# Attention with pooled keys and a gated MLP: the main keys of the values, loaded 64 keys by two heads per transfer in place of two heads by 64 keys

## The chip, the cores and the metric

The kernel runs on one core of one Trainium2 chip. The time is the device time of one execution in microseconds, as the median of several executions; three of the kernel before are shown. Beside these there is one profiled execution, from which every duration below comes.

## The reference, cut to what matters

Eight batches (B) of eight heads (H) with 576 tokens (S) of 64 numbers (D), all float32. Keys and values are first averaged over groups of 8 tokens, which leaves 72 pooled keys for each head; attention of the 576 queries over the 72 pooled keys gives a 576 x 512 array for each batch, and a gated MLP follows it.

```python
k_p = k.reshape(B, H, Sp, pool, D).mean(axis=3)          # pool = 8, Sp = 72
v_p = v.reshape(B, H, Sp, pool, D).mean(axis=3)
scores = scale * np.matmul(q, k_p.transpose(0, 1, 3, 2))
attn = softmax(scores)
x = np.matmul(attn, v_p)                                 # then (B, S, H * D) = (8, 576, 512)
h = np.maximum(x @ w_in, 0.0)                            # 1024 columns
u, v = h[..., :512], h[..., 512:]
v_n = (v - mean(v)) / sqrt(var(v) + 1e-06)
v_s = np.einsum('ts,bsd->btd', w_spatial, v_n) + b_spatial[None, :, None]
return (u * v_s) @ w_out
```

## The kernel before, in words

The work of one batch is cut into named steps, each a Python generator that records a few instructions at a time: K (load and pool the keys), V (the same for the values), Q (load queries), S (scores and softmax), T and Y (bring the softmax weights into the layout of the next product), A (weights times values, into `xT`), and for the MLP v, u, s and o. The long string `ORDER` at the top of the file lists which step records its next piece. That list alone sets the order of the instructions on every engine and of the transfers on the queue: each engine runs its instructions in this order, and nothing overtakes. Batches overlap: while the MLP of one batch runs on PE, K, V, Q, S and T of the next ones run on the other engines.

All transfers are issued by the sync engine (SP; its rows read SPq) in that one order. The ones that matter here:

- V of batches 2 to 7 (`att_values`, from line 471): the 64 main pooled keys of the eight heads are 8 x 64 rows of 8 x 64 numbers, so 512 numbers or 2 KB each, contiguous in memory for one pooled key. They come in as two tiles `st` of 128 partitions x 2 x 512 from a ring of three buffers that K, V and the weights share. Partition i * 64 + p, slot e holds pooled key p of head 4r + 2i + e. Each tile is filled by two transfers (line 477), so there are four for a batch and 24 in all, of 256 KB each. POOL then adds the eight rows of each group (L307, L312).
- K of batches 2 to 7 (line 422): the same sizes; a transfer takes 64 keys by two heads into 128 partitions, partition 2 * key + head.
- The eight left-over pooled keys of each head (`load_rest`, line 335): 64 partitions, 128 KB.
- Q (line 536), 72 KB in each transfer, four for a pair of heads.
- T goes through memory: DVE transposes the weights into X and XR (L676, L680), SP writes them to `xd` and `xdr` (L683, L686) and reads them back as `pt` (L690) and `pt_r` (L694); ACT and DVE then split `pt_r` into `pt_rr` (L637, L639), and PE multiplies (A, L751 and L754). Y does the same for the last 64 tokens, through `xdl` and `xdlr` (L727 to L737).
- o: ACT copies a result into one of two buffers `ob` (L895), SP stores it (L898). Step v uses the same two buffers for a temporary (`t2`, L824).

Batches 0 and 1 load their keys and values in another way (`first_keys`, `first_values`), which the change leaves alone.

Of the kernel before, what the change touches and what calls it, by code (L numbers as in the profile page):

```python
# [99 lines left out]
def pooled_attention_gmlp(ctx: ExitStack, tc: tile.TileContext, q, k, v, w_in, w_sp, b_sp, w_out, out):  # L100
    nc = tc.nc
# [17 lines left out]
    KM = P // 2  # L119
# [51 lines left out]
    def ring(tag, bufs, shape, dt, name, pool=pl):  # L171
        return pool.tile(shape, dt, name=name, tag=tag, bufs=bufs)
# [130 lines left out]
    def pool_sum(st, dst, eng=nc.vector):  # L303

        w = POOL * D // 2
        while w > D:
            eng.tensor_tensor(st[:, :, :w], st[:, :, :w], st[:, :, w:2 * w], op=ALU.add)  # L307
            w //= 2
        x, y = st[:, :, :w], st[:, :, w:2 * w]
        if len(dst.shape) == 4:  # L310
            x, y = (t.unsqueeze(2).broadcast_to(dst.shape) for t in (x, y))
        eng.tensor_tensor(dst, x, y, op=ALU.add)  # L312

    def pool_half(sts, alt):

        if "%" in alt:
            for st in sts:
                x = st[:, :, :POOL * D // 2]
                eng = nc.vector if "^" in alt else nc.gpsimd
                eng.tensor_tensor(x, x, st[:, :, POOL * D // 2:], op=ALU.add)  # L320
                yield

    def pool_pe(st, dst, alt):

        m, n = dst.shape[0], POOL // 2 if "%" in alt else POOL
        for j in range(n):
            nc.tensor.matmul(dst, lhsT=ident[:m, :m], rhs=st[:, :, j * D:(j + 1) * D], start=j == 0, stop=j == n - 1)

    def ps_pool():
        return ps_big()[:, :(NG + 1) * D].rearrange("p (g d) -> p g d", d=D)  # L330

    def load_rest(src):

        st = ring("kvr", 1, [2 * RR, 1, POOL * D], F32, "st_r")
        nc.sync.dma_start(out=st[:, 0, :], in_=src[:, KM * POOL:, :].rearrange("h (s j) d -> h s (j d)", j=POOL))
        return st

    def rest_engine(alt, pe):

        if pe:  # L340
            return nc.vector if "~" in alt else nc.gpsimd if "!" in alt else None
        return nc.gpsimd if alt else nc.vector
# [43 lines left out]
    def first_values(b, vp, vq):  # L386

        rows = v[b, :, :KM * POOL, :].rearrange("(j i e) (p f) d -> i j p e (f d)", j=2, i=2, f=POOL // 2)
        sts = []
        for h in range(2):  # L390
            sts.append(ring("kv", 3, [P, NG, POOL // 2 * D], F32, "st"))
            for j in range(2):
                nc.sync.dma_start(out=sts[h][:, 2 * j:2 * j + 2, :], in_=rows[h, j])
            yield
        rest = load_rest(v[b])
        yield
        acc = ps_pool()
        for j in range(POOL // 2):
            for h in range(2):
                nc.tensor.matmul(acc[h * KM:(h + 1) * KM, :NG, :], lhsT=pairs, rhs=sts[h][:, :, j * D:(j + 1) * D],  # L400
                                 start=j == 0, stop=j == POOL // 2 - 1)
        yield
        pool_pe(rest, acc[:2 * RR, NG:, :], "")
        yield
        nc.scalar.copy(vp, acc[:, :NG, :])
        nc.scalar.copy(vq, acc[:2 * RR, NG:, :])
        yield
# [54 lines left out]
    def att_values(t, b, alt=""):  # L462

        eng = nc.gpsimd if alt else nc.vector
        vp = ring("vp", 2, [P, NG, D], F32, "vp")
        vq = pl.tile([2 * RR, 1, D], F32, name="vq", tag="vq")
        vr_s = pl.tile([RR, NG, 2, D], F32, name="vr_s", tag="vr_s")
        t["v"] = vp, vr_s
        if b < PE_B:
            yield from first_values(b, vp, vq)  # L470
        else:
            sts, g2 = [], [slice(2 * r, 2 * r + 2) for r in range(2)]
            keys = v[b, :, :KM * POOL, :].rearrange("(r i e) (p j) d -> r e i p (j d)", r=2, i=2, j=POOL)
            for r in range(2):
                sts.append(ring("kv", 3, [P, 2, POOL * D], F32, "st"))
                for e in range(2):
                    nc.sync.dma_start(out=sts[r][:, e, :], in_=keys[r, e])
                yield
            st = load_rest(v[b])
            yield  # L480
            pe = "^" in alt or "%" in alt
            yield from pool_half((*sts, st)[:2 if rest_engine(alt, True) else 3], alt)
            for r in range(2):
                if pe:
                    acc = acc if r else ps_pool()
                    pool_pe(sts[r], acc[:, g2[r], :], alt)
                else:
                    pool_sum(sts[r], vp[:, g2[r], :], eng)
                yield
            by = rest_engine(alt, pe)  # L490
            if by is not None:
                pool_sum(st, vq, by)
            else:
                pool_pe(st, acc[:2 * RR, NG:, :], alt)
            if pe:
                yield
                nc.scalar.copy(vp, acc[:, :NG, :])
                if by is None:
                    nc.scalar.copy(vq, acc[:2 * RR, NG:, :])
                yield  # L500
        for j in range(2):
            rs = slice(j * RR, (j + 1) * RR)
            nc.vector.tensor_tensor(vr_s[:, 2 * j:2 * j + 2, :, :].rearrange("p i e d -> p (i e) d"),
                                    vq[rs].broadcast_to([RR, 4, D]),
                                    mask[rs].unsqueeze(2).broadcast_to([RR, 4, D]), op=ALU.mult)
# [258 lines left out]
    def attention(b):  # L764

        t = {}
        st = {
            "K": lambda **alt: att_keys(t, b, **alt),
            "KT": lambda **alt: att_keys_t(*t["k"], **alt) if b >= PE_B else iter(()),
            "V": lambda **alt: att_values(t, b, **alt),  # L770
            "W": lambda: att_values_split(*t["v"]),
        }
        for g in range(NG):
            st[f"Q{g}"] = lambda g=g, **alt: att_q(t, b, g, **alt)
            st[f"S{g}"] = lambda g=g, **alt: att_softmax(t, b, g, **alt)
        for j in range(NG // 2):
            st[f"T{j}"] = lambda j=j, **alt: att_pt(t, b, j, **alt)
            st[f"Y{j}"] = lambda j=j, **alt: att_pt_l(t, b, j, **alt)
            for half in range(2):
                st[f"A{half}{j}"] = lambda half=half, j=j: att_av(t, half, j)  # L780
        return st, t
# [185 lines left out]
```

## Time and profile before

| | us |
|---|---|
| median of 3 executions | 621.76 |
| lowest and highest | 621.35, 624.94 |
| the profiled execution | 623.88 |
| its span | 622.1 |
| PE busy within the span | 541.8 |
| mean granted clock of PE | 0.942 |

PE is the TensorE matmul, PEld its weight load, DVE the VectorE, ACT the ScalarE, POOL the GpSimd. The profiled execution's time is its span and 1.8 us around it. PEclk and "granted clock" are shares of full speed: 1.00 is 2.4 GHz and 0.50 is 1.2 GHz. "DMA share" is the mean busy share of the core's 16 DMA engines. In rows of a timeline, the figure in square brackets is how long the engine was idle just before the row, and the name behind the arrow is what ended that idle time.

### The profile page before, as it was taken

Reading aid. Unit: us, or ns where it says so; the run is one execution under the profiler, and the core shown is the slowest. Engines: PE = TensorE matmul, PEld = TensorE weight load, DVE = VectorE, ACT = ScalarE, POOL = GpSimd, SP = SyncE. Lnnn points to the kernel's source line nnn. Section 1 sums busy time; section 2 is a strip of 40 time slices with the busy share of each in tenths; the row PEclk is TensorE's granted clock in tenths of the full one; section 3 lists DMA queues with packets and bytes.
Section 4 is the critical chain, followed back from the end, with each engine's and each line's share of the span. In section 5 each row is a group of like instructions: output and inputs, shape, how many; then the busy total and the mean of one; then the engine's idle time right before and its main releaser. Section 6 shows DMA issues by size and latency. Waiting matters only on the chain.

```text
span 622.1 us, 12097 instructions
## 1 busy us (share of the span) xinstructions
PE 541.8 (87%) x4514; PEld 465.6 (75%) x4514; DVE 330.1 (53%) x723; ACT 269.7 (43%) x875; POOL 286.8 (46%) x389
## 2 busy tenths in 40 slices
PE   4899999917963888969799999989769999999998
PEld 3678888916942677858688888768659888988996
DVE  4898989805730437735683576444255654234210
ACT  3589685403720225614545356144144534333322
POOL 2354778815740734843656644224515644221331
PEclk9999999977976797998899999989969999999999
DMA  8986535423144544332645623352232032200002
GB/s 219 271 240 148 133 73 120 103 77 72 45 113 115 152 133 88 92 99 93 142 101 151 148 47 83 110 141 67 77 100 80 3 105 90 70 18 17 35 2 84
DMA packets 122587, 63.12 MB, mean 101 GB/s; under 512 B 81184, under 2 KB 106272, under 8 KB 122528
## 3 DMA queue, kind: packets, MB, share of 16 engines
q1 hardware_dynamic: 122528, 62.35, 38.4%
q8 instruction: 35, 0.57, 0.4%
q14 instruction: 24, 0.20, 0.1%
HBM read 44.92 MB, written 17.40 MB: 100 GB/s over the span
## 4 chain that ended last, share of the span: by engine, by line
PE 65%; DMA 11%; DVE 7%; SPq 6%; POOL 5%; ACT 5%; issue 1%; ACTq 0%; DVEq 0%; POOLq 0%
PE mm L865 14%; PE mm L804 13%; PE mm L891 12%; PE mm L847 12%; DMA out<-ob 4%; PE s_ps L611 2%; PE mm L820 2%; PE tp L751 2%; DMA pt_r<-xdr 2%; PE tp L754 2%; DMA qt<-in_q 2%; ACT e L587 2%; SPq L536 2%; DMA st<-in_k 1%; SPq L694 1%
## 5 line engine op out<-in xcount | busy, mean ns | idle before, releaser
L847 PE MATMUL mm<-xT,win_h 128*128 128x256 f32 (+1 forms) x512 | 104.9, 299 | 4.9 <-DVE vv L827 4.6
L879 POOL TENSOR_TENSOR gT<-g,gT 128x256 fp32r<-128x256 f32 x64 | 47.6, 750 | 125.1 <-ACT gT L876 125.1
L804 PE MATMUL mm<-win_h,xT 128*128 128x512 f32 x256 | 85.7, 417 | 13.6 <-ACT ob L895 9.3
L847 PEld LDWEIGHTS mm<-xT,win_h 128*128 128x128 f32 x512 | 84.6, 191 | 8.0 <-DVE vv L827 5.1
L865 PE MATMUL mm<-wT_h,vn_h 128*128 128x320 f32 (+1 forms) x256 | 77.8, 304 | 9.0 <-ACT ob L895 9.0
L891 PE MATMUL mm<-wout_h,gT 128*128 128x512 f32 (+1 forms) x264 | 80.7, 388 | 0.0
L865 PE MATMUL mm<-wT_l,vn_h 128*128 128x320 f32 (+1 forms) x256 | 77.1, 301 | 0.0
L865 PE MATMUL mm<-wT_h,vn_l 128*128 128x320 f32 (+1 forms) x256 | 77.0, 301 | 0.0
L847 PE MATMUL mm<-xT,win_l 128*128 128x320 f32 (+1 forms) x256 | 76.0, 297 | 0.0
L870 DVE TENSOR_TENSOR g<-mm,ru 128x320 f32<-128x320 f32 (+1 forms) x64 | 28.4, 453 | 82.3 <-PE mm L867 56.9
L804 PEld LDWEIGHTS mm<-win_h,xT 128*128 128x128 f32 x256 | 49.9, 201 | 25.3 <-ACT ob L895 9.5
L594 POOL TENSOR_TENSOR e<-e,rs 128x720 f32<-128x720 f32 (+1 forms) x32 | 41.2, 1287 | 49.9 <-DVE rs L592 47.5
L791 POOL TENSOR_TENSOR rstd<-rstd,neg_half 128x1 f32<-128x1 f32 (+1 forms) x40 | 24.7, 623 | 81.3 <-DVE rstd L789 81.2
L865 PEld LDWEIGHTS mm<-wT_h,vn_h 128*128 128x128 f32 x256 | 49.8, 195 | 10.3 <-ACT ob L895 9.7
L587 ACT ACTIVATE e<-s_ps,mx 128x72 f32<-128x72 f32 x174 | 52.8, 334 | 10.7 <-DVE mx L573 10.6
L891 PEld LDWEIGHTS mm<-wout_h,gT 128*128 128x128 f32 x264 | 48.2, 188 | 9.8
L804 PE MATMUL mm<-win_l,xT 128*128 128x512 f32 x128 | 52.9, 413 | 0.0
L785 DVE BATCH_NORM_STATS2 st<-vv 128x6 f32<-128x512 f32 (+1 forms) x40 | 27.2, 681 | 48.0 <-ACT vv L808 43.8
L814 POOL TENSOR_TENSOR vn_l<-vv,vn_h 128x512 fp32r<-128x512 f32 x32 | 42.0, 1328 | 21.7 <-ACT vn_h L812 21.7
L307 POOL TENSOR_TENSOR st<-st 128x512 f32<-128x512 f32 (+1 forms) x44 | 45.1, 1025 | 13.8 <-DMA st<-in_k 8.6
L891 PE MATMUL mm<-wout_l,gT 128*128 128x512 f32 (+1 forms) x132 | 51.4, 389 | 0.0
L865 PEld LDWEIGHTS mm<-wT_h,vn_l 128*128 128x128 f32 x256 | 49.8, 195 | 0.5
(171 smaller groups left out, 1142.7 us busy)
## 6 DMA issues: line engine op xcount, KB each, us to landing
st<-in_k SPq DMA_DIRECT2D x32, 256.0 KB
st<-in_v SPq DMA_DIRECT2D x32, 256.0 KB
out<-ob SPq DMA_DIRECT2D x31, 256.0 KB
qt<-in_q SPq DMA_DIRECT2D x104, 72.0 KB
xd<-X SPq DMA_DIRECT2D x24, 256.0 KB
pt<-xd SPq DMA_DIRECT2D x24, 256.0 KB
stw<-in_moe_w_in SPq DMA_DIRECT2D x8, 512.0 KB
st<-in_moe_w_out SPq DMA_DIRECT2D x4, 512.0 KB
```

The costliest lines, as they stand in the source:

```text
L307: eng.tensor_tensor(st[:, :, :w], st[:, :, :w], st[:, :, w:2 * w], op=ALU.add)
L587: nc.scalar.activation(em[:, h, :], sv[:, h % 2, h // 2, :], AF.Exp, bias=mx[:, h:h + 1], scale=QK, accum_out=sm[:, h:h + 1])
L594: nc.gpsimd.tensor_tensor(em, em, rs.unsqueeze(2).broadcast_to([P, n, SP]), op=ALU.mult)
L785: nc.vector.bn_stats(st6[:m], vv[:m])
L791: nc.gpsimd.tensor_tensor(rstd[:m], rstd[:m], neg_half[:m], op=ALU.pow)
L804: nc.tensor.matmul(a, lhsT=xT[:, i, o + c * P:o + (c + 1) * P], rhs=w[:, i, DH:], start=(i == 0 and j == 0), stop=(i == NK - 1 and j == 2))
L814: nc.gpsimd.tensor_tensor(t["vn_l"][:, c, :], vv, f32(t["vn_h"][:, c, :]), op=ALU.subtract)
L847: nc.tensor.matmul(a, lhsT=w[:, i, d * P:(d + 1) * P], rhs=xT[:, i, o + ts.start:o + ts.stop], start=(i == 0 and j == 0), stop=(i == NK - ...
L865: nc.tensor.matmul(a, lhsT=x[:, c, ds], rhs=y[:, c, ts], start=(c == 0 and j == 0), stop=False)
L870: nc.vector.tensor_tensor(g, a, t["ru"][:, d, ts], op=ALU.mult)
L879: nc.gpsimd.tensor_tensor(dst[:, d, 1, at:at + m], g[:, o:o + m], f32(dst[:, d, 0, at:at + m]), op=ALU.subtract)
L891: nc.tensor.matmul(a, lhsT=src[:, i, x, at:at + m], rhs=w[:, i, cols], start=(i == 0 and j == 0), stop=(i == ND - 1 and j == 2))
```

## The change

The two transfers that fill a tile of values no longer take one slot e each for all 128 partitions; each takes one half of the partitions (one i) with both slots.

```diff
             for r in range(2):
                 sts.append(ring("kv", 3, [P, 2, POOL * D], F32, "st"))
-                for e in range(2):
-                    nc.sync.dma_start(out=sts[r][:, e, :], in_=keys[r, e])
+                for i in range(2):
+                    nc.sync.dma_start(out=sts[r][i * KM:(i + 1) * KM], in_=keys[r, :, i].rearrange("e p f -> p e f"))
                 yield
```

KM is 64. On the side of the memory a transfer was a loop over 2 heads, in it 64 keys, in it 512 numbers, and went to 128 partitions of 512 numbers. Now it is a loop over 64 keys, in it 2 heads, in it 512 numbers, and goes to 64 partitions of 2 x 512 numbers. Bytes (256 KB), the number of transfers (24), the pieces of 2 KB and the place of every number in the tile are the same.

On PE, DVE, ACT and POOL no instruction and no place in the order differs. (Near 270 us and 285 us PE gets two buffers of the ring `mm` the other way round: a group of L865 there waits for DVE and no longer for ACT, the L450 behind it the reverse, and two rows of L751 exchange their waits for PE and DVE.) On SP the order is the same too; only the shape of L477 differs. The queue of SP around the first V of this kind (batch 2), before: shapes are partitions x pieces x numbers.

```order
L536 DMA qt<-in_q 32x18x32 x4
L477 DMA st<-in_v 128x1x512 x2
L690 DMA pt<-xd 128x4x128 x2
L477 DMA st<-in_v 128x1x512 x2
L694 DMA pt_r<-xdr 32x4x128 x2
L536 DMA qt<-in_q 32x18x32 x8
L335 DMA st_r<-in_v 64x1x512
```

The same place in the change:

```order
L536 DMA qt<-in_q 32x18x32 x4
L477 DMA st<-in_v 64x2x512 x2
L690 DMA pt<-xd 128x4x128 x2
L477 DMA st<-in_v 64x2x512 x2
L694 DMA pt_r<-xdr 32x4x128 x2
L536 DMA qt<-in_q 32x18x32 x8
L335 DMA st_r<-in_v 64x1x512
```

Nothing moved; `pt_r` still stands behind four transfers of values. A little further on, four transfers of values (batch 3) stand together; in the change this piece of SP's queue reads:

```order
L737 DMA pt_r<-xdlr 32x2x32 x2
L477 DMA st<-in_v 64x2x512 x4
L727 DMA xdl<-XL 4x16x128 x2
L730 DMA xdlr<-XLR 64x32
L898 DMA out<-ob 128x512
L683 DMA xd<-X 8x16x512
```

Here too only the shape of L477 is another (before, 128x1x512).

## Rows read from the trace of the kernel before

**Rows 1.** The head of the page: busy time, share of the span and instructions of each engine.

```profile
PE 541.8 (87%) x4514; PEld 465.6 (75%) x4514; DVE 330.1 (53%) x723; ACT 269.7 (43%) x875; POOL 286.8 (46%) x389
```

**Rows 2.** PE in order of time: the rows with more than 1 us of idle time before them, from 100 us on (start, duration, operation; in brackets the idle time and what ended it).

```profile
143.93 0.48 PE L450 MATMUL tp<-ident,kp 128*128 128x128 f32 x1 [17.13 <-ACT ru L850]
181.96 0.58 PE L865 MATMUL mm<-wT_h,vn_h 128*128 128x256 f32 x1 [6.11 <-ACT ob L895]
201.44 1.08 PE L751 MATMUL tp<-pt,vp 64*64 64x256 f32 x2 [10.65 <-DMA pt<-xd]
204.94 0.70 PE L751 MATMUL tp<-pt,vp 64*64 64x256 f32 x3 [2.42 <-DVE xT L183]
235.94 0.58 PE L847 MATMUL mm<-xT,win_h 128*128 128x256 f32 x1 [4.64 <-DVE vv L827]
272.62 0.39 PE L865 MATMUL mm<-wT_h,vn_h 128*128 128x256 f32 x1 [1.39 <-ACT ob L895]
276.01 0.33 PE L450 MATMUL tp<-ident,kp 128*128 128x128 f32 x1 [1.36 <-POOL kp L312]
279.65 0.48 PE L451 MATMUL tp<-ident,kr 128*128 128x128 f32 x1 [3.32 <-POOL kr L312]
305.32 0.69 PE L804 MATMUL mm<-win_h,xT 128*128 128x512 f32 x1 [3.74 <-DVE g L870]
399.92 0.42 PE L865 MATMUL mm<-wT_h,vn_h 128*128 128x320 f32 x1 [1.52 <-ACT ob L895]
414.65 0.58 PE L754 MATMUL tp<-pt_rr,vr 96*128 96x256 f32 x1 [1.41 <-DVE pt_rr L639]
456.75 0.79 PE L804 MATMUL mm<-win_h,xT 128*128 128x512 f32 x1 [9.32 <-ACT ob L895]
```

**Rows 3.** Busy time of each engine, the granted clock of PE (the column 0.50), DMA share and GB/s in the eight stretches after 100 us in which PE had half its clock: the first, the fifth, the sixth, and the sum of the eight (start:end, length, then PE, PEld, DVE, ACT, POOL).

```profile
131.40:148.50 17.10, 4.57 (x23) 3.35 (x27) 2.12 (x5) 3.03 (x8) 2.85 (x3) 0.50 0.36 79
...
278.20:285.00 6.80, 5.35 (x79) 5.12 (x83) 1.67 (x4) 1.93 (x6) 2.08 (x4) 0.50 0.30 95
305.50:308.90 3.40, 3.40 (x9) 2.63 (x10) 3.30 (x4) 3.40 (x18) 3.18 (x6) 0.50 0.28 42
...
sum 71.60, PE 37.11 PEld 30.56 DVE 25.57 ACT 21.62 POOL 22.28; mean PE 4.64 PEld 3.82 DVE 3.20 ACT 2.70 POOL 2.79
```

**Rows 4.** The same columns for three long stretches in which no transfer of L477 is under way (34.00:116.00, 305.30:376.00 and the one shown), and the sum of the three.

```profile
456.70:619.00 162.30, 162.25 (x1064) 143.24 (x1064) 66.12 (x149) 62.82 (x173) 55.53 (x78) 0.98 0.18 53
sum 315.00, PE 312.73 PEld 270.77 DVE 188.00 ACT 158.15 POOL 155.84; mean PE 104.24 PEld 90.26 DVE 62.67 ACT 52.72 POOL 51.95
```

**Rows 5.** The same columns; the last two are the DMA share and GB/s. One stretch with transfers of L477 (values) under way, and one with four transfers of L422 (keys) under way.

```profile
160.00:166.00 6.00, 6.00 (x30) 4.95 (x29) 5.53 (x7) 4.02 (x18) 4.92 (x5) 1.00 0.13 51
204.50:208.00 3.50, 3.06 (x14) 2.33 (x15) 2.06 (x5) 1.65 (x7) 3.44 (x7) 0.50 0.86 224
```

**Rows 6.** SP in order of time: start, time in which it issued, line, out<-in, number of transfers.

```profile
116.26 1.17 SPq L477 DMA_DIRECT2D st<-in_v  x2
117.53 6.01 SPq L690 DMA_DIRECT2D pt<-xd  x2
123.64 5.96 SPq L477 DMA_DIRECT2D st<-in_v  x2
129.65 3.71 SPq L694 DMA_DIRECT2D pt_r<-xdr  x2
...
155.22 9.99 SPq L477 DMA_DIRECT2D st<-in_v  x4
165.31 7.33 SPq L727 DMA_DIRECT2D xdl<-XL  x2
...
174.04 0.73 SPq L898 DMA_DIRECT2D out<-ob  x1
174.87 0.59 SPq L683 DMA_DIRECT2D xd<-X  x1
...
204.23 2.54 SPq L422 DMA_DIRECT2D st<-in_k  x4
```

**Rows 7.** ACT and DVE in order of time: three rows whose results the transfers of rows 6 from 165 us on carry, or that free their buffer (L895 for `out`, L676 for `xd`, L557 for the next `qt`).

```profile
159.94 0.64 ACT L895 COPY ob<-mm 128x512 f32<-128x512 f32 x1
164.32 1.13 DVE L676 STREAM_TRANSPOSE X<-e 128x512 f32<-128x512 f32 x1
171.45 0.20 DVE L557 STREAM_TRANSPOSE pt_q<-qt 128x64 f32<-128x64 f32 x1
```

**Rows 8.** The chain of work that ended last, in order of time: the transfers in it from 130 us to 300 us (start of the part that the chain followed, its length, what).

```profile
132.82 10.05 DMA pt_r<-xdr
...
174.04 7.20 DMA out<-ob
...
199.64 3.25 DMA pt_r<-xdr
...
223.88 10.60 DMA out<-ob
...
265.60 7.59 DMA st<-in_k
```

**Rows 9.** Busy time in two of PE's waits of rows 2, columns as in rows 3.

```profile
271.20:279.60 8.40, 2.39 (x17) 1.94 (x16) 2.37 (x5) 2.40 (x7) 5.96 (x10) 0.91 0.15 36
301.60:305.30 3.70, 0.00 (x0) 0.00 (x0) 3.56 (x11) 2.53 (x16) 0.35 (x1) 1.00 0.79 175
```

## The prediction

> **What bounds the kernel now.** I read the head of the page first: PE is busy for 541.8 us of 622.1, no other engine for more than 330.1 [rows 1]. So PE sets the time, and what can be won is what PE loses. It loses it in two forms.
>
> The first is idle time. From 100 us on, twelve waits of more than 1 us add up to 63.0 us: 17.13 + 6.11 + 10.65 + 2.42 + 4.64 + 1.39 + 1.36 + 3.32 + 3.74 + 1.52 + 1.41 + 9.32 [rows 2]. The second is the clock. Eight stretches of 71.6 us together ran at 0.50, which is 1.2 GHz, and each begins in or just behind one of these waits (131.4 us lies in the wait that ends at 143.93, 305.5 us right behind the one that ends at 305.32) [rows 2, 3]. PE was busy for 37.1 us in them [rows 3]; at 2.4 GHz that work takes half, so the clock costs 18.6 us. Together that is 81.6 us.
>
> Next I asked whether the waits have one cause. In 315 us in which no transfer of values is under way, PE was idle for 315.0 - 312.7 = 2.3 us, or 0.7% [rows 4]. All twelve waits lie between 126 and 457 us, where the values of batches 2 to 7 come in. So I looked at these transfers.
>
> In a stretch with only values under way the DMA share is 0.13 and 51 GB/s flow; with four transfers of keys under way it is 0.86 and 224 GB/s [rows 5]. A share of 0.13 is 2 of 16 engines, and the values are a loop over 2 heads, the keys one over 64 keys. Each transfer of values thus holds two engines for 262,144 B / 51 GB/s = 5.1 us, where one of keys of the same size takes 1.17 us.
>
> SP shows what that does to the others. Four transfers of keys were issued in 2.54 us, 0.64 each; four of values took 9.99 us, and the two small `xdl` behind them 7.33 us [rows 6]. SP does not wait for data there: what `out` at 174.04 carries was ready at 160.58, what `xd` carries at 165.45, and the buffer of the next Q was free at 171.65 [rows 6, 7]. The queue itself is full. And what is issued lands late, since every transfer has pieces on the two engines too: `pt_r` at 132.82 + 10.05 = 142.87, `out` at 174.04 + 7.20 = 181.24 and at 223.88 + 10.60 = 234.48, K at 265.60 + 7.59 = 273.19, where `pt_r` in a clear queue took 3.25 us [rows 8]. These landings stand just ahead of the ends of PE's waits [rows 2].
>
> **The change, part by part.** It removes nothing and adds nothing on PE, DVE, ACT and POOL; on SP 24 transfers keep their place, bytes and number. The buffers of `mm` that change places make one L865 near 271 us wait for DVE and not for ACT; I put that at 0, between -1.39 us (it was held by ACT for that long [rows 2]) and as much the other way.
>
> What changes is how many engines carry a transfer. The trace shows no transfer of exactly the new form. Its loop (64 keys, in it 2 heads) is that of K, so I take 1.17 us for 5.1. The bounds are 5.1 us (still two engines) and 1.17.
>
> What each wait becomes, with its cover:
>
> Batch 2, 17.13 us. PE ran out of work at 143.93 - 17.13 = 126.80 and went on 1.06 us after `pt_r` landed. In the change SP issues two values from 116.26, two `pt`, two values and two `pt_r`, at 0.64 us each: the last `pt_r` at about 120.7, in the clear there at 124.0. The four transfers' bytes need 4 x 1.17 = 4.7 us, from about 117.5 to 122.2. I take 125 for the landing and 126.1 for the restart: the wait goes, with 0.7 us to spare. The 9.32 us at the end have the same order of transfers behind them and are taken the same way.
>
> Batch 3, 6.11 us. SP issues its four values by 155.22 + 2.54 = 157.8, three small ones by 159.7, then `out` when ACT is ready at 160.58; it lands by 164. PE ran out of work at 175.85: gone, with 12 us to spare.
>
> 10.65 and 2.42 us behind it. `xd` goes out at 165.5, the four Q from 171.65 (their buffer) to 174.2, then `pt`, which lands by 178.1. PE, earlier by the 6.11, wants it at 190.79 - 6.11 = 184.7: gone, with 6 us to spare. What ended the 2.42 is the `pt_r` of the same group.
>
> 4.64 us: `out` at 223.88 lands by 227.2, and PE ran dry at 231.30: gone.
>
> 1.39 + 1.36 + 3.32 and 3.74 us: the late K and a late Q go, but a second engine stands behind them. In the first 8.4 us POOL has 5.96 us of work, in the last 3.70 us DVE has 3.56 [rows 9]. K would land some 4 us earlier and POOL start earlier by as much; whether that is all of the wait the rows don't say. I keep half: (6.07 + 3.74) / 2 = 4.9 us, and with it half of what the clock costs behind them, (5.35 + 3.40) / 4 = 2.2 us [rows 3]. Bounds 0 and 14.2.
>
> 1.52 and 1.41 us stand right behind `out` and `pt_r` like the others and go.
>
> Where waits go, so does the half clock behind them. Outside the twelve there was none after 100 us.
>
> The sum: 623.88 - 63.0 - 18.6 = 542.3 us if all of it goes; plus 4.9 + 2.2 = **549.4** against the profiled execution. That execution lies 2.1 us above the median of those shown (621.76), so against the median I say **547**.
>
> One rule speaks against the full gain. By the rows, K writes 128 partitions at 224 GB/s, and I gave the new transfers, which write 64, the same rate. The Trainium skill (SBUF — State Buffer, Door 1: The DMA port swizzle) has it that partitions 0 to 63 lie behind half of the ports that all 128 reach, so 64 partitions get the bandwidth of 32, and that two transfers into the two halves do not add up. The trace before cannot show whether that holds here. As a mechanism of this kernel it is the rival below, priced at half of K's rate.
>
> **The rivals.**
>
> Half rate into half of the partitions. A transfer takes 2.34 us, four take 9.4. At batch 2 the bytes are through at 126.9, `pt_r` lands near 128.5, PE starts at 129.6 and waits 2.8 us, and runs some 3.4 us at half clock behind it (as behind the wait of 3.74), 1.7 us. The other places have 4 us and more to spare. That is 4.5 us twice (batch 2 and the last), so 556. For it: nothing in the trace. Against it: nothing either. 0.15.
>
> Another wait takes the place of those removed. PE then finds `kp`, `xT` or the softmax late, since ACT, DVE and POOL had PE's idle time to catch up in. For it: rows 9. Against it: in the rest they kept up with PE though DVE was busy in 188 of 315 us [rows 4]. If half of the 81.6 us stays: 583, against the median 581. 0.20.
>
> No change: the transfer is still carried by two engines, the share stays at 0.13, and the time is 622. Against it: K's form [rows 5]. By the Trainium skill (DMA: Bandwidth & Descriptors, Why a DMA increments its semaphore by 16 and not by 1) the number of engines is the largest up to 16 that divides the slowest dimension of both sides; by it the old form has 2 and the new one 16. The share of 0.13 agrees for the old. 0.03.
>
> Slower: a transfer is carried by one engine, since its 64 partitions or its 4 KB of a partition are not cut as K's are. It then takes 10.3 us, and 24 of them 123 us more. Today's 123 us made 63 us of idle time, so as much more comes on top, with 18 us for the clock: about 703. It decides as soon as the share in a stretch with values alone lies below 0.13. Nothing speaks for it but that the form is new. 0.02.
>
> **How the numbers follow.** My forecast has 0.60, with 540 to 555 as its own range; half rate 0.15, another wait 0.20, no change 0.03, slower 0.02. The predicted time is that of the first, 547. The lower end, 539, is the sum with nothing kept, 542.3, less the 2.1 us to the median, and a little for scatter. The upper end, 571, takes in the half rate and the part of the third case in which less than a third of the 81.6 us stays; beyond it lie some 0.13 of that case and the last two, 0.18 together. About 1% is what a measurement of this kernel can tell from no change: faster 0.95, same 0.03, slower 0.02.
>
> **What the profile of the change would show.** Up to 116 us the two traces should agree. The share in a stretch with values alone should be 0.8 or more where it was 0.13; if it is near 0.4, the half rate is right. SP should issue two values and the two transfers behind them in about 2.6 us, not 7. The `pt_r` of batch 2 should land near 125 us, not 142.87. PE should have no wait over 3 us behind 100 us, its granted clock should be near 1.00 throughout, and its busy time about 541.8 - 18.6 = 523 us. I am wrong if the share rises and PE still waits: then rows with POOL, DVE or ACT as what ended the wait name the next bound.

## The result and the profile after

The changed kernel took 544.92 us (median of 4 runs, 544.19 to 547.05), the kernel before beside it 621.56. The ratio is 0.8764, 95% interval 0.8722 to 0.8807. The forecast was 547 us, with a range of 539 to 571.

The page's head after the change, span and busy time of each engine, to be held against [rows 1]:

```profile
span 542.4 us, 12097 instructions
PE 523.2 (96%) x4514; PEld 451.7 (83%) x4514; DVE 329.9 (61%) x723; ACT 269.3 (50%) x875; POOL 287.9 (53%) x389
```

The number of instructions is the same. PE's busy time fell by 541.8 - 523.2 = 18.6 us and its idle time from 80.3 to 19.2 us; the two make up the whole 79.7 us between the spans. PE's granted clock is 1.00 throughout, so 18.6 is what the half clock had cost.

PE from 100 us on after the change, all rows with more than 0.5 us of idle time before them, against the twelve of [rows 2]:

```profile
149.41 0.39 PE L865 MATMUL mm<-wT_h,vn_h 128*128 128x256 f32 x1 [0.62 <-ACT ru L850]
179.81 0.33 PE L451 MATMUL tp<-ident,kr 128*128 128x128 f32 x1 [1.22 <-POOL kr L312]
259.23 0.65 PE L751 MATMUL tp<-pt,vp 64*64 64x256 f32 x5 [1.35 <-ACT ru L850]
298.07 0.50 PE L804 MATMUL mm<-win_h,xT 128*128 128x512 f32 x1 [0.58 <-DVE xT L183]
```

No wait is longer than 1.35 us, and two are over 1 us where there were twelve. What made them go shows on SP, in the stretch of batch 2 that [rows 6] showed of before (start, duration, issue):

```profile
115.92 1.35 SPq L477 DMA_DIRECT2D st<-in_v  x2
117.37 1.08 SPq L690 DMA_DIRECT2D pt<-xd  x2
118.56 1.52 SPq L477 DMA_DIRECT2D st<-in_v  x2
120.13 1.07 SPq L694 DMA_DIRECT2D pt_r<-xdr  x2
121.30 5.31 SPq L536 DMA_DIRECT2D qt<-in_q  x8
...
136.11 3.41 SPq L477 DMA_DIRECT2D st<-in_v  x4
139.62 1.16 SPq L727 DMA_DIRECT2D xdl<-XL  x2
```

The two `pt` behind the first values are issued in 1.08 us where they took 6.01, the four values of batch 3 in 3.41 where they took 9.99, and the two `xdl` behind them in 1.16 where they took 7.33. The same `pt_r` in the chain that ended last, against [rows 8] (start, length, what):

```profile
120.76 4.70 DMA pt_r<-xdr
```

It lands at 125.46 and not at 142.87. The busy times, clock, DMA share and GB/s in a stretch with values under way (two small `xdl` and an `xdlr`, 72 KB together, flow in it too), against [rows 5], and in two long stretches in which PE had waited before:

```profile
139.00:143.00 4.00, 4.00 (x25) 3.70 (x24) 3.88 (x6) 2.97 (x18) 3.94 (x5) 1.00 1.06 252
```

```profile
126.00:300.00 174.00, 170.11 (x1506) 146.60 (x1506) 116.66 (x245) 87.39 (x309) 117.74 (x164) 1.00 0.58 140
300.00:455.00 155.00, 155.00 (x1130) 135.68 (x1129) 87.44 (x199) 74.27 (x245) 70.80 (x99) 1.00 0.35 88
```

252 GB/s flow where 51 did; without the small transfers it is still at least 234. From 300 to 455 us PE does not idle at all, and DVE, ACT and POOL have time to spare in both stretches. PE idles for 3.9 us of the first.

### The profile page after: what moved, and what is told of

The parts are those of the page before. It is cut to its first block, busy times and chain, and to the rows that moved or that the text cites. A ratio compares the mean times of both kernels' runs of the same rounds, so it can differ in the third digit from the quotient of the medians.

```text
span 542.4 us, 12097 instructions
## 1 busy us (share of the span) xinstructions
PE 523.2 (96%) x4514; PEld 451.7 (83%) x4514; DVE 329.9 (61%) x723; ACT 269.3 (50%) x875; POOL 287.9 (53%) x389
## 4 chain that ended last, share of the span: by engine, by line
PE 71%; DVE 11%; DMA 5%; ACT 5%; SPq 4%; POOL 2%; issue 1%; DVEq 0%; ACTq 0%; POOLq 0%
PE mm L891 15%; PE mm L865 15%; PE mm L847 14%; PE mm L804 12%; PE s_ps L611 3%; PE mm L820 2%; PE tp L751 2%; DMA qt<-in_q 2%; PE tp L754 2%; SPq L536 2%; ACT e L587 1%; DMA pt_r<-xdr 1%; DVE mx L571 1%; PE mm L866 1%; PE mm L867 1%
## 5 line engine op out<-in xcount | busy, mean ns | idle before, releaser
L804 PE MATMUL mm<-win_h,xT 128*128 128x512 f32 x256 | 80.8, 396 | 0.6 <-DVE xT L183 0.6
L865 PE MATMUL mm<-wT_h,vn_h 128*128 128x320 f32 (+1 forms) x256 | 75.7, 296 | 0.6 <-ACT ru L850 0.6
L865 PE MATMUL mm<-wT_l,vn_h 128*128 128x320 f32 (+1 forms) x256 | 75.3, 294 | 0.0
L865 PE MATMUL mm<-wT_h,vn_l 128*128 128x320 f32 (+1 forms) x256 | 75.3, 294 | 0.0
L804 PEld LDWEIGHTS mm<-win_h,xT 128*128 128x128 f32 x256 | 46.8, 188 | 10.9 <-DVE xT L183 1.0
L814 POOL TENSOR_TENSOR vn_l<-vv,vn_h 128x512 fp32r<-128x512 f32 x32 | 42.3, 1337 | 23.1 <-ACT vn_h L812 23.1
L876 ACT ACTIVATE gT<-g 128x256 fp32r<-128x256 f32 x64 | 26.4, 415 | 53.6 <-DVE g L870 52.2
L804 PE MATMUL mm<-win_l,xT 128*128 128x512 f32 x128 | 50.7, 396 | 0.0
L865 PEld LDWEIGHTS mm<-wT_h,vn_h 128*128 128x128 f32 x256 | 48.1, 188 | 1.3 <-ACT ru L850 0.8
L865 PEld LDWEIGHTS mm<-wT_h,vn_l 128*128 128x128 f32 x256 | 48.1, 188 | 0.5
L847 PEld LDWEIGHTS mm<-xT,win_l 128*128 128x128 f32 x256 | 48.2, 188 | 0.0
```

The source lines that it names most:

```text
L804: nc.tensor.matmul(a, lhsT=xT[:, i, o + c * P:o + (c + 1) * P], rhs=w[:, i, DH:], start=(i == 0 and j == 0), stop=(i == NK - 1 and j == 2))
L814: nc.gpsimd.tensor_tensor(t["vn_l"][:, c, :], vv, f32(t["vn_h"][:, c, :]), op=ALU.subtract)
L847: nc.tensor.matmul(a, lhsT=w[:, i, d * P:(d + 1) * P], rhs=xT[:, i, o + ts.start:o + ts.stop], start=(i == 0 and j == 0), stop=(i == NK - ...
L865: nc.tensor.matmul(a, lhsT=x[:, c, ds], rhs=y[:, c, ts], start=(c == 0 and j == 0), stop=False)
L876: nc.scalar.activation(dst[:, d, 0, at:at + m], g[:, o:o + m], AF.Copy)
```

## The experiments

The theory: each old transfer holds two DMA engines for 5.1 us; what SP issues behind it also has pieces on these two, so it lands late, and SP's queue fills; PE waits for what is late, and the half clock follows the wait. The rivals: PE waited for the values themselves; the cost is the same for each transfer; only SP's blocked queue matters; the transfers into 64 partitions are themselves slow.

**One batch at a time.** Six kernels, each with the old form in one batch only (here batch 2; the others with 3, 4, 5, 6, 7 in its place):

```diff
-                    nc.sync.dma_start(out=sts[r][i * KM:(i + 1) * KM], in_=keys[r, :, i].rearrange("e p f -> p e f"))
+                    if b == 2:
+                        nc.sync.dma_start(out=sts[r][:, i, :], in_=keys[r, i])
+                    else:
+                        nc.sync.dma_start(out=sts[r][i * KM:(i + 1) * KM], in_=keys[r, :, i].rearrange("e p f -> p e f"))
```

> The four transfers of values of batch 2 go back to two heads by 64 keys; batches 3 to 7 stay as changed. My theory (two engines are held for 5.1 us by each old transfer, so what is queued behind it on SP lands late, and PE waits for that): the price is that of batch 2's own place in the trace of before, the wait of 17.13 us and the half clock behind it, about 2.3 us, so 545 + 19.4 = 564 us. Rival, a cost that is the same for each of the 24 transfers, since PE waits for the values themselves: a sixth of the 77 us between before and after, so 558 us for any batch.

> The same for the four transfers of batch 4 alone. My theory: the waits behind its transfers in the trace of before are 10.65, 2.42 and 4.64 us, and 5.35 us of half clock's cost belongs to them, 23.1 in all: about 568 us. The rival with an equal cost for every batch: 558 us.

> The same for the four transfers of batch 6 alone. My theory: only the waits of 1.52 and 1.41 us and about 1.7 us of half clock stand behind them, 4.6 in all: about 549.5 us. The rival with an equal cost for every batch: 558 us. This place separates the two best.

> The four transfers of batch 3 alone go back to two heads by 64 keys. By the rows of before its place has the wait of 6.11 us and 2.0 us of half clock, 8.1 in all, so 553 us. But batch 4 alone cost 14.6 us where its rows gave 23.1, and its wait for pt was 4.96 us where before had 10.65: if the rest of that wait was batch 3's, still in line then, batch 3 costs 8.1 + 8.5 = 16.6 us, 561.5 us. The equal cost for every batch gives 558.

> The four transfers of batch 5 alone go back to two heads by 64 keys. By the rows of before: waits of 1.39, 1.36, 3.32 and 3.74 us and 4.4 us of half clock, 14.2 in all, so 559 us, if the transfers explain the whole of them. If half belongs to POOL and DVE, as the prediction had it, 7.1 us, so 552.

> The four transfers of batch 7 alone go back to two heads by 64 keys. By the rows of before: the wait of 9.32 us and 2.8 us of half clock, 12.1 in all, so 557 us. If the six batches add up, the price here is what is left of the 76.6 us between before and after: 76.6 - 17.6 - 14.6 - 4.9 less batches 3 and 5.

| old form in batch | us, median | over 544.92 | by the rows of before | ratio to before, 95% |
|---|---|---|---|---|
| 2 | 562.48 | 17.6 | 19.4 | 0.9028 to 0.9088 |
| 3 | 559.08 | 14.2 | 8.1 | 0.8989 to 0.9048 |
| 4 | 559.54 | 14.6 | 23.1 | 0.8986 to 0.9048 |
| 5 | 560.14 | 15.2 | 14.2 | 0.9011 to 0.9068 |
| 6 | 549.85 | 4.9 | 4.6 | 0.8830 to 0.8904 |
| 7 | 556.11 | 11.2 | 12.1 | 0.8932 to 0.9045 |

The six prices add up to 77.7 us, and before and after are 76.6 us apart. All six lean on the same 544.92, whose own uncertainty is some 2.5 us, so the sum is good to about 15 us; within that the batches add up. An equal cost of 12.8 us for each is out: batch 6 costs 4.9 and batch 2 17.6, as their places say. The long wait of batch 2 and that of batch 7 come back in the kernels with that batch alone (17.13 and 9.32 us in [rows 2]; in these kernels lines stand 3 lower than before):

```profile
144.43 0.69 PE L450 MATMUL tp<-ident,kp 128*128 128x128 f32 x2 [17.27 <-ACT ru L853]
```

```profile
389.34 1.22 PE L807 MATMUL mm<-win_h,xT 128*128 128x512 f32 x2 [8.96 <-ACT ob L898]
```

Batches 3 and 4 together cost 28.8 where the rows gave 31.2, but I had shared them out wrongly. The rows of PE at the place of the 10.65 us show why, first in the kernel with batch 4 alone, then with batch 3 alone:

```profile
168.97 1.08 PE L754 MATMUL tp<-pt,vp 64*64 64x256 f32 x2 [4.99 <-DMA pt<-xd]
172.57 1.12 PE L754 MATMUL tp<-pt,vp 64*64 64x256 f32 x6 [2.52 <-DVE xT L183]
```

```profile
164.53 0.58 PE L868 MATMUL mm<-wT_h,vn_h 128*128 128x256 f32 x1 [5.07 <-ACT ob L898]
175.68 0.61 PE L754 MATMUL tp<-pt,vp 64*64 64x256 f32 x2 [1.57 <-DMA pt<-xd]
179.38 1.12 PE L754 MATMUL tp<-pt,vp 64*64 64x256 f32 x6 [3.09 <-DVE xT L183]
```

The wait of 10.65 us for `pt` [rows 2] was made by two batches: alone, batch 4 makes 4.99 of it and batch 3 1.57. The other 4.1 us came only with both, so single waits do not add up as the prices do. A wait can have its cause one batch earlier.

Batch 5 alone, the same view:

```profile
228.21 0.39 PE L868 MATMUL mm<-wT_h,vn_h 128*128 128x256 f32 x1 [1.13 <-ACT ob L898]
231.59 0.33 PE L450 MATMUL tp<-ident,kp 128*128 128x128 f32 x1 [1.35 <-POOL kp L312]
235.23 0.48 PE L451 MATMUL tp<-ident,kr 128*128 128x128 f32 x1 [3.31 <-POOL kr L312]
...
261.39 1.22 PE L807 MATMUL mm<-win_h,xT 128*128 128x512 f32 x2 [5.29 <-DVE g L873]
```

The waits of 1.39, 1.36, 3.32 and 3.74 us of before come back one by one (the last as 5.29), with POOL and DVE named as what ended three of them, though only four transfers differ from the changed kernel, which has none of these waits in this size. Ahead of these three POOL and DVE stood idle themselves, until K and Q landed, and from there to PE's start they worked without a gap. Their rows in the kernel with batch 5 alone, then in the kernel before:

```profile
228.92 2.09 POOL L307 TENSOR_TENSOR st<-st 128x512 f32<-128x512 f32 x2 [7.74 <-DMA st<-in_k]
256.93 0.71 DVE L559 STREAM_TRANSPOSE qT<-qt 128x512 f32<-128x512 f32 x1 [8.80 <-DMA qt<-in_q]
```

```profile
273.32 2.10 POOL L307 TENSOR_TENSOR st<-st 128x512 f32<-128x512 f32 x2 [7.99 <-DMA st<-in_k]
300.87 0.71 DVE L556 STREAM_TRANSPOSE qT<-qt 128x512 f32<-128x512 f32 x1 [7.25 <-DMA qt<-in_q]
```

POOL and DVE were late because what they work on was late, and the trace of before had these rows already.

**More old transfers, that nobody waits for.** Values in the new form, and behind each pair two transfers of the old form into unused memory:

```diff
                 for i in range(2):
                     nc.sync.dma_start(out=sts[r][i * KM:(i + 1) * KM], in_=keys[r, :, i].rearrange("e p f -> p e f"))
+                for e in range(2):
+                    spare = dr.tile([P, POOL * D + D], F32, name=f"spare{b}{r}{e}")
+                    nc.sync.dma_start(out=spare[:, :POOL * D], in_=keys[r, e])
```

> The values come in as changed (64 keys by two heads), but behind each pair of them SP issues two more transfers of the same bytes in the old form, two heads by 64 keys, into memory that nobody reads: 24 transfers and 6.3 MB of reading and writing more, which no engine waits for. My theory (two engines are held, and what is queued behind lands late): PE waits for pt_r, out and K again as before, about 620 us, a little more at batch 3 and 4 since the values come first and the queue then fills. Rival, PE lost its time because the values themselves came late: they come early here, so 545 to 555 us.

Measured: 638.18 us, ratio to before 1.0279 (1.0249 to 1.0308). PE's waits, added up by line (what waits, what ended it: us in total, times, longest):

```profile
PE tp L450 <- ACT ru L853: 19.7, 1, 19.7
PE mm L807 <- ACT ob L898: 12.5, 1, 12.5
PE mm L868 <- ACT ob L898: 12.1, 2, 8.4
PE tp L754 <- DMA pt<-xd: 11.3, 1, 11.3
PE mm L807 <- DVE g L873: 6.9, 1, 6.9
PE mm L850 <- DVE vv L830: 5.2, 1, 5.2
```

These are the waits of [rows 2] at the same operations, each longer: 19.7 for 17.13, 12.5 for 9.32, 11.3 for 10.65, 6.9 for 3.74, 5.2 for 4.64. That PE waited for the values themselves is out. In the second pair of a batch the new values, too, are issued behind old transfers here, but from 116 us on no wait of an engine, in this kernel or the one before, is put down to a transfer of values. In the kernel before, those put down to transfers are for `pt_r`, `out`, `pt`, K, Q and `xd`, the longest of them ACT's:

```profile
ACT pt_rr L637 <- DMA pt_r<-xdr: 35.7, 2, 19.9
ACT ob L895 <- DMA out<-ob: 27.6, 4, 10.1
```

In a stretch in which little but the added transfers is under way, the share and the flow are those of two engines, as in [rows 5]:

```profile
170.00:174.00 4.00, 4.00 (x34) 3.96 (x33) 1.94 (x4) 3.28 (x13) 2.10 (x3) 1.00 0.13 51
```

The run adds bytes as well as held engines. At 252 GB/s the four added transfers of a batch would take some 4.2 us, and the wait at batch 2 is 19.7, so the bytes alone hardly make it; a run with the same bytes added in the new form was not made. I had said "a little" above 620 and it was 17 us more. I put that down to the values' new transfers, which still stand in line, now in front of the old ones; no run separates it.

**The dose: 4, 8 and 16 engines.** The same 256 KB by loops over 4 heads by 32 keys (here), over 8 heads by 16 keys, and over 64 keys by two heads into all 128 partitions:

```diff
-                for i in range(2):
-                    nc.sync.dma_start(out=sts[r][i * KM:(i + 1) * KM], in_=keys[r, :, i].rearrange("e p f -> p e f"))
+                for e in range(2):
+                    n = 2 * r + e
+                    h, s = n * 32 // KM * 4, n * 32 % KM
+                    nc.sync.dma_start(out=sts[r][:, e, :], in_=v[b, h:h + 4, s * POOL:(s + 32) * POOL, :].rearrange(
+                        "h (p j) d -> h p (j d)", j=POOL))
```

> Each transfer of values carries 4 heads by 32 keys, 256 KB as before, into 128 partitions; by the reading of the trace its slowest loop has 4 and it should be carried by 4 engines and take about 2.6 us. Values land in other partitions than the reference has them in. My theory: four take about 10.2 us where two of them and two others stand ahead of pt_r of batch 2, so its last bytes are through at about 127.8 us, it lands near 129 us and PE waits some 3 to 4 us there and as much at batch 7, with the half clock behind: 550 to 560 us. Rival, the price goes with the time of a transfer (5.1 us costs 77, so 2.6 us costs (2.6 - 1.2)/(5.1 - 1.2) of it, 28 us): 573 us.

> Each transfer of values carries 8 heads by 16 keys into 128 partitions, so 8 engines, about 1.3 us. Values land in other partitions than the reference has them in. My theory: nothing is late any more, 545 to 548 us. Rival with the price in proportion: 547 us. If 8 engines do not suffice, above 550.

> The values as 64 keys by two heads into all 128 partitions, the form of K's transfers. The keys come to stand in other partitions than the reference has them in, so the values of the attention are paired with wrong keys; work and times of the engines are those of the change. My theory (only the number of engines mattered, and the four transfers of a batch use both halves of the partitions together): the same time as the change within 1%, 545 us. Rival, the transfers into 64 partitions run at half of the rate that 128 would give and cost time at batches 2 and 7: 2 to 9 us less than the change, 536 to 543 us.

Measured: 571.67 us (0.9158 to 0.9218 of before), 552.1 (0.8834 to 0.8908) and 544.37 (0.8732 to 0.8785). A stretch with values under way in each, in that order (columns as above; some small transfers flow in them too):

```profile
150.00:154.00 4.00, 4.00 (x25) 3.71 (x24) 3.95 (x4) 2.38 (x15) 3.94 (x6) 1.00 0.26 101
```

```profile
145.00:148.00 3.00, 3.00 (x20) 2.82 (x19) 2.95 (x3) 1.91 (x11) 2.94 (x4) 1.00 0.52 195
```

```profile
139.00:142.00 3.00, 3.00 (x20) 2.87 (x20) 2.92 (x5) 2.77 (x17) 2.94 (x5) 1.00 0.84 267
```

Shares of 0.13, 0.26 and 0.52 of 16 engines with 51, 101 and 195 GB/s for loops over 2, 4 and 8 heads: here the number of engines is that of the slowest loop. The Trainium skill (DMA: Bandwidth & Descriptors, Why a DMA increments its semaphore by 16 and not by 1) counts the engines in the same way, up to 16; these three shares agree with it, and 1.06 and 0.84 for the two loops over 64 keys fit all 16.

My own figures failed in both: 550 to 560 for 4 heads, where the proportional rival (573) came closer, and 545 to 548 for 8 heads, where the rival's 547 failed too. The transfers of the chain that ended last show the slip: the `pt_r` of batch 2, first with 4 heads, then with 8.

```profile
125.40 8.52 DMA pt_r<-xdr
```

```profile
120.51 9.35 DMA pt_r<-xdr
```

With 4 heads it lands at 133.92 and not at my 129. The four values alone need 4 x 2.6 = 10.4 us; I had left out the time from issue to the first bytes and the two `pt` between them, which stand in the same line. How much of the 5 us each of these took was not measured. PE waited 8.48 us there and not 3 to 4. At batch 7, where I had forecast as much, no wait came; PE waited 3.6, 2.9 and 3.3 us at the places of the 10.65, 2.42 and 3.32 us of [rows 2]. With 8 heads the landing of `pt_r` is at 129.86 and PE waited 4.18 us: eight engines do not suffice. There is no slack at batch 2: the landing is 8.46 and 4.40 us later than in the change (125.46), and PE waits 8.48 and 4.18.

The form with 128 partitions takes what the change takes, 544.37 against 544.92 with overlapping intervals: the half of the partitions costs nothing that can be told apart in this kernel.

**The same form for K.** Values as changed, K's 24 transfers as two heads by 64 keys:

```diff
-                nc.sync.dma_start(out=sts[r][:, e, :], in_=keys[r, e, :KM, :, :])
+                nc.sync.dma_start(out=sts[r][:, e, :], in_=keys[r, e, :KM, :, :].rearrange("s a f -> a s f"))
```

> The values as changed, but the 24 transfers of K of batches 2 to 7 as two heads by 64 keys. The keys come to stand in other partitions than the reference has them in, so scores and values are paired wrongly; the work of the engines is the same. My theory (any transfer on SP's queue that only two engines carry makes what is queued behind it late): the time rises again by some tens of us though the values are fast, 575 to 625 us, with waits of PE behind K, Q and pt. Rival, something of the values' own place in the program caused the waits: 545 to 555 us.

Measured: 619.81 us, 0.9971 of before (0.9949 to 0.9993). PE's waits, added up by line:

```profile
PE tp L450 <- POOL kp L312: 16.6, 3, 10.2
PE mm L847 <- DVE vv L827: 12.6, 1, 12.6
PE mm L847 <- DVE g L870: 6.5, 2, 4.9
PE mm L865 <- ACT ob L895: 6.1, 1, 6.1
PE tp L451 <- POOL kr L312: 5.7, 2, 3.2
```

Nearly the whole gain is lost again, mostly at other places: nothing about values is special. Here PE also waits for what the slow transfers carry: POOL stood idle for 44.3 us until tiles `st` of K landed. So this run does not separate K's own lateness from that of what is queued behind it; the added transfers above, which nobody waits for, do.

**Another queue.** The old form, issued by ACT:

```diff
-                for i in range(2):
-                    nc.sync.dma_start(out=sts[r][i * KM:(i + 1) * KM], in_=keys[r, :, i].rearrange("e p f -> p e f"))
+                for e in range(2):
+                    nc.scalar.dma_start(out=sts[r][:, e, :], in_=keys[r, e])
```

> All 24 transfers of values go back to two heads by 64 keys, on two engines, but ACT issues them, at the same place of its own order, so they stand in ACT's queue and SP's queue holds only the others. Two theories of how the old form hurts: if it was that SP's queue is full and SP cannot issue, SP is free here and most of the gain stays, 550 to 565 us, the rest for the engines that are shared; if it was that every other transfer has pieces on the two held engines and they wait there behind the values, a second queue helps only as far as the two queues take turns on an engine, and pt_r, out and K still land late: 580 to 620 us. ACT waits at these places for the values' buffers, which may add some us by itself.

Measured: 608.6 us, ratio 0.982 (0.9789 to 0.9852). SP at batch 2, where it now issues no values:

```profile
116.14 0.98 SPq L694 DMA_DIRECT2D pt_r<-xdr  x2
117.22 20.82 SPq L536 DMA_DIRECT2D qt<-in_q  x8
```

ACT at batch 3:

```profile
150.03 10.19 ACTq L477 DMA_DIRECT2D st<-in_v  x4
160.27 0.38 ACT L850 ACTIVATE ru<-mm 128x256 f32<-128x256 f32 x1 [9.67 <-issue]
```

Two transfers of the chain that ended last:

```profile
172.48 18.61 DMA st<-in_v
...
380.19 12.05 DMA out<-ob
```

The eight Q take SP 20.82 us though no value stands in its queue (5.31 after the change), and an `out` that SP issues at 380.19, 1 us after ACT has issued two values, takes 12.05 us to land. It is the two engines that are shared, not SP's queue alone. A full queue is a price of its own: ACT stands 10.19 us at its four issues, and PE waits 7.08 us for the `ru` behind them. So this run does not say how much of before's loss was SP's full queue and how much late landing; the 11.5 us that it gained are a sum of both and of ACT's stalls. The Trainium skill (DMA: Bandwidth & Descriptors, Issuing engines are not separate DMA queues) says that several issuing engines save only the time of issuing, since all end up on the same 16 DMA engines; the 12.05 us agree.

## Why the prediction was right

**What bounds the kernel.** Right. 18.6 us for the clock was the measured fall of PE's busy time to the digit, and PE's idle time fell by 61.1 us where the twelve waits were 63.0.

**The cause.** Right: the waits and their half clock come back with the 24 transfers, batch by batch in sum, though batches 3 and 4 share theirs otherwise than their places said, and they come back when two engines are held by transfers that nobody reads.

**How many engines carry the new form.** Right: a share of 1.06 and 252 GB/s where K's rate of 224 was taken. The last `pt_r` was put at 120.7 for its issue and 125 for its landing; it was 120.76 and 125.46. The first two values and the two `pt` behind them were put at 2.6 us of issue and took 2.5.

**What is kept at the 1.39, 1.36, 3.32 and 3.74 us.** This is the step that was mis-sized: "I keep half", 4.9 + 2.2 = 7.1 us, since POOL and DVE had work up to the end of these waits [rows 9]. None of the four is left among the rows over 0.5 us after the change; the 63.0 - 61.1 = 1.9 us that the whole kernel kept are small waits at other places. Batch 5 alone brought all four waits back. Being busy until PE starts showed only that POOL and DVE were the last link, not that they had started on time: in the trace of before POOL had stood idle for 7.99 us until K landed, and DVE for 7.25 us until Q did.

**From the sum to the median.** The sum of 549.4 was 5.2 us too high against the profiled 544.19 us: the 7.1 us of that term, less the 1.9 kept elsewhere. The 2.1 us taken off for the median did not carry over: the profiled execution after lies 0.7 below its own median. 549.4 - 5.2 + 0.7 = 544.9; that the forecast of 547 came so near is in part luck, since the two errors had opposite signs.

**The rivals.** Half rate into half of the partitions: shown wrong by 252 GB/s, where it had half of 224, and by the form with 128 partitions, which is not faster. Another wait in the place of those removed: wrong, 1.35 us is the longest. No change, and one engine: wrong by the share. The exchanged buffers of `mm`, put at 0, show no wait: the only L865 among the rows over 0.5 us waits 0.62 us at 149.41, far ahead of that place.

## What to carry to other kernels

Look for a low DMA share together with a full queue, and count the slowest loop of each transfer: a transfer over 2 heads held two engines for 5.1 us where sixteen needed about 1, and its price was paid by whatever was issued behind it, for the values not by what they carry. Reorder the loops of the pattern before moving transfers to another queue. When an engine is busy right up to the end of a wait, ask when its own input landed before calling it the next bound.

## What the runs showed that was not expected

The transfers into 64 partitions have a share of 1.06 at 252 GB/s, those into 128 a share of 0.84 at 267: the same bytes hold the engines longer, and packets overlap (a share over 1), but the flow is nearly the same. The Trainium skill (SBUF — State Buffer, Door 1: The DMA port swizzle and "Can I just issue two DMAs to hit both halves?") has 64 partitions at half of the ports, and two transfers into the two halves at 6% over one. No run here writes into one half alone, so that 6% is not tested; what the runs show is that four transfers in a row into alternate halves flow nearly as fast as four into all 128 partitions, and that the kernel takes the same time.

At batch 2 a small lengthening costs more than its bytes. With 8 engines a transfer of values takes 262,144 B / 195 GB/s = 1.34 us, with 16 it takes 1.04, so four cost some 1.2 us more. Yet the landing moves by 129.86 - 125.46 = 4.4 us. Where the other 3 us come from was not taken apart.
